# MoE of a sliding-window attention in 18 blocks of 256 tokens, two column tiles per slot; masks and relayouts of the first 16 slots on VectorE

## The chip, the cores and the metric

The kernel runs on one core of a Trainium2 chip. TensorE (PE) multiplies matrices into PSUM; VectorE (DVE), ScalarE (ACT) and GpSimd (POOL) work element by element; SyncE (SP) stores the output. Each engine carries out its own instructions in the order in which they were issued to it, and waits where an operand or a buffer isn't ready. The metric is the device time in microseconds (us); the kernel before takes 369.12 us, the median of three runs.

## What is computed

```python
# q, k, v: [8, 8, 576, 64] float32; w_in: [512, 2048]; w_out: [2048, 512]
scores = np.matmul(q, k.transpose(0, 1, 3, 2)) / np.sqrt(64)
scores = np.where(np.abs(pos[:, None] - pos[None, :]) <= 32, scores, -1e9)
attn   = softmax(scores)                       # over the last axis
x = np.matmul(attn, v).transpose(0, 2, 1, 3).reshape(4608, 512)
h = x @ w_in
g = np.where(h >= 1, h, np.where(h <= -1, 0.0, (h + 1) ** 2 / 4))
out = g @ w_out                                # [4608, 512] float32
```

There are 8 batches of 8 heads and 576 tokens. The window of 32 leaves, for each block of 64 keys, 128 queries (96 at the ends).

## The kernel before

**Attention.** Two heads of one batch are stacked on the 128 partitions and called a pair i (32 of them, four per batch); two pairs are loaded together and called m (16 of them, two per batch). GpSimd issues the loads, which also turn float32 into bfloat16: `load_qk(m)` for q and k, `load_v(m)` into a ring of four buffers vz. q, and k of m = 0 to 3 (`LONG = 4`), come in long rows; a copy (`relay`) then brings them into the order that TensorE's transposes want (tile qj or kj), `tpose(m, t)` transposes a part (t = 0, 1 for q, 2, 3 for k) into PSUM and copies it out as qT or kT, and for those k `zfill` copies kT into kz, where the two heads of a pair lie beside zeros. From m = 4 on, k is loaded by four DMAs of short runs in an order that needs neither: its transposes are copied from PSUM straight into kz, four copies by VectorE for each of t = 2 and 3.

`scores(i, g, eng)` does one of three groups of key blocks of a pair: matmuls (tile sc), ScalarE's exponential into pt, and a product with the band mask on the engine `eng`. `pv(i, half)` sums pt (tile dn) and multiplies it with vz (tile nm) for one half of 288 tokens, takes 1/dn as exp(-ln dn) on ScalarE, and leaves a product on VectorE for the next slot, which writes 288 columns of xT. Batch 0 is done for the first half before slot 0.

**MoE.** It runs in 9 blocks of TB = 512 tokens, each of 16 slots. A slot multiplies 128 rows of h, four matmuls of 512 columns, into PSUM (tile hp, two buffers); ScalarE makes rr = relu(h/2 + 1/2), VectorE the larger of hp and rr and then min(rr, 1) times that, which is g (tile gT). Block 0 alone takes its tokens in two halves of 256: its slots do two row tiles of 256 columns each. From slot 16 on every slot also does four matmuls of w_out for the block before (tile op, 16 of them sum up one output tile of 128 tokens, copied out by ScalarE and stored by SP). Sixteen slots at the end have only these.

**What sets the order.** It is written out by hand. A table `ev` says in which slot a score group ("s"), a transpose ("t") or a pv half ("v") stands; `loads` says in which slot GpSimd issues a load, and `rel` puts a relayout one slot ahead of its first transpose. Inside a slot the order is: loads, products left over from pv, hp and its three elementwise operations, scores, op, relayouts, transposes, zfill, pv. Up to slot 5 the masks are VectorE's, from slot 6 on GpSimd's (`eng = V if a < 6 else P`); all relayouts and refills inside the slots are GpSimd's. A GpSimd load waits for the load issued eight before it, and for its buffer.

Of the kernel before, what the change touches and what calls it, by code (L numbers as in the profile page):

```python
# [15 lines left out]
def kernel(  # L16
# [68 lines left out]

    LONG = 4

# [71 lines left out]
    load_qk(2)  # L159
    load_qk(3)  # L160
    load_v(2)


# [11 lines left out]
    def tpose(m, t, early=False):  # L175
# [26 lines left out]
    def zfill(m, g, early=False):  # L202
        for h in range(2):
            r = slice(64 * h, 64 * h + 64)
            copy = nc.gpsimd.tensor_copy if not early else nc.scalar.copy if h else nc.vector.tensor_copy
            copy(kz[2 * (m % 2) + g][r, :, h], kT[m][r, g].rearrange("d (c r) -> d c r", r=64))  # L206

    pt = {}

    def scores(i, g, eng):  # L210
# [108 lines left out]
    for n, a in enumerate([8, 9, 10, 11, 13, 14, 15, 15]):  # L319
        at(a, "v", 4 + n // 2, n % 2)  # L320
    for b in range(2, B):
        a0 = 16 * (b - 1)
        early = b == 2
        for n in range(4):
            for g in range(3):
                at(a0 + (1, 1, 2)[g] if early and n == 0 else a0 + 4 * n + g - 2, "s", 4 * b + n, g)
            at(a0 + 4 * n + 1 + (1 if early and n == 0 else 0), "v", 4 * b + n, 0)
            at(a0 + 4 * n + 3, "v", 4 * b + n, 1)
        for t in range(4):
            at((15, 15, 16, 16)[t] if early else a0 - 10 + 2 * t, "t", 2 * b, t)  # L330
            at(a0 + 1 + t if early else a0 - 2 + 2 * t, "t", 2 * b + 1, t)
    slots = sorted(set(ev) | set(range(16 * NB + 16)))
    rel, zf = {}, {}
    for a, es in ev.items():
        for e in es:
            if e[0] == "t" and (e[2] == 0 or e[2] == 2 and e[1] < LONG):
                rel.setdefault(slots[slots.index(a) - 1], []).append((e[1], e[2] // 2))
            if e[0] == "t" and e[2] == 3 and e[1] < LONG:
                zf.setdefault(a, []).append(e[1])
# [89 lines left out]
```

## Time and profile before

| | |
|---|---|
| median of 3 runs | 369.12 us (369.08 to 369.27) |
| profiled execution | 368.57 us, of which its span of instructions 366.8 us |
| TensorE busy | 323.5 us, 88% of the span |
| VectorE, ScalarE, GpSimd busy | 268.8, 226.4, 181.9 us |
| mean granted TensorE clock | 0.972 of 2.4 GHz |

A busy share is an average over stages with different limits, so the stages are read apart: the timeline of an engine shows when each operation starts, how long it takes, and behind which engine's work it waited; windows give the busy time of each engine in a stretch. The chain that ended last follows the end of the program back through what released each step. A granted clock of 0.50 is TensorE's lower level, 1.2 GHz.

### The profile page before, as it was taken

The numbers are of one execution on the slowest core, as the hardware profiler recorded it, in microseconds if no ns is written. First come the engines' busy times: TensorE is split into PE (matmuls) and PEld (weight loads), VectorE is DVE, ScalarE is ACT, GpSimd is POOL, SyncE is SP. The second block draws the span as 40 slices with busy tenths as digits, with TensorE's granted clock in tenths as the row PEclk, the third lists the DMA queues.
The fourth block names the chain that finished last, engine by engine and source line by source line (L and its number), as shares of the span: only waits on it lengthen the run. The fifth ranks groups of instructions, "written<-read, shape, count | busy, mean of one in ns | idle before, by whom it ended". The sixth has DMA issues, their size and how long they took to land.

```text
span 366.8 us, 6093 instructions
## 1 busy us (share of the span) xinstructions
PE 323.5 (88%) x2205; PEld 184.8 (50%) x2240; DVE 268.8 (73%) x489; ACT 226.4 (62%) x449; POOL 181.9 (50%) x229
## 2 busy tenths in 40 slices
PE   2577276488999999899999999999999999999995
PEld 1456165345555555455555555555555544444442
DVE  6569363556887888788888797979797788878810
ACT  7968354456776776677676868686866653443321
POOL 8935988939484849384949494824223200000000
PEclk9989878879999999999999999999999999999999
DMA  7999999759193949393929090900000011001012
GB/s 104 187 209 185 204 60 94 66 32 116 34 98 63 82 74 109 47 91 64 116 42 126 30 126 29 128 30 29 31 29 30 29 42 46 29 37 51 29 59 84
DMA packets 79612, 28.16 MB, mean 77 GB/s; under 512 B 66784, under 2 KB 74464, under 8 KB 79584
## 3 DMA queue, kind: packets, MB, share of 16 engines
q0 software_dynamic: 74400, 18.36, 53.6%
q1 hardware_dynamic: 5184, 9.44, 6.9%
q8 instruction: 17, 0.28, 0.3%
q14 instruction: 11, 0.09, 0.1%
HBM read 36.70 MB, written 9.44 MB: 126 GB/s over the span
## 4 chain that ended last, share of the span: by engine, by line
PE 77%; POOL 10%; ACT 4%; DVE 3%; issue 3%; DMA 2%; POOLq 0%; ACTq 0%
PE op L380 33%; PE hp L363 31%; PE tp L186 4%; PE nm L246 4%; PE sc L218 3%; POOL pt L223 3%; POOL kn L95 3%; PE dn L236 2%; PE dn L237 2%; DMA kn<-in_k_dram 2%; POOL kz L206 1%; POOL qn L100 1%; DVE pt L223 1%; POOL vz L105 1%; ACT rc L251 1%
## 5 line engine op out<-in xcount | busy, mean ns | idle before, releaser
L363 PE MATMUL hp<-xT,w_in 128*128 128x512 bf16 (+1 forms) x621 | 151.5, 366 | 3.5 <-DVE xT L255 2.2
L380 PE MATMUL op<-w_out,gT 128*128 128x512 bf16 x560 | 143.4, 380 | 0.9
L367 ACT ACTIVATE rr<-hp 128x512 f32<-128x512 f32 x144 | 86.0, 597 | 83.9 <-PE hp L363 72.9
L368 DVE TENSOR_TENSOR hp<-hp,rr 128x512 f32<-128x512 f32 x144 | 100.7, 699 | 45.7 <-ACT rr L367 43.7
L223 POOL TENSOR_TENSOR pt<-pt,maskp 128x352 bf16<-128x352 bf16 (+2 forms) x84 | 73.8, 884 | 94.5 <-ACT pt L222 94.3
L369 DVE SCALAR_TENSOR_TENSOR gT<-rr,hp 128x512 bf16<-128x512 f32 x144 | 99.0, 687 | 5.0
L363 PEld LDWEIGHTS <-w_in 128*128 128x128 bf16 x640 | 60.1, 101 | 42.8 <-issue 1.7
L380 PEld LDWEIGHTS <-gT 128*128 128x128 bf16 x576 | 53.5, 98 | 52.3 <-issue 1.3
L222 ACT ACTIVATE pt<-sc 128x352 bf16<-128x352 f32 (+2 forms) x96 | 44.0, 468 | 2.2 <-PE sc L218 2.1
L255 DVE TENSOR_TENSOR xT<-nm,rc 128x288 bf16<-128x288 f32 x64 | 29.0, 455 | 17.9 <-ACT rc L251 17.8
L250 ACT ACTIVATE lr<-dn 128x288 f32<-128x288 f32 x64 | 26.5, 414 | 18.6 <-PE dn L237 18.6
L218 PEld LDWEIGHTS <-kz 128*128 128x128 bf16 x288 | 23.2, 101 | 24.9 <-issue 4.9
L95 POOL DMA_DIRECT2D kn<-in_k_dram x48 | 35.7, 767 | 0.0
L218 PE MATMUL sc<-qT,kz 128*128 128x128 bf16 (+1 forms) x288 | 30.8, 222 | 4.9 <-ACT pt L222 2.7
L198 ACT COPY qT<-tp 128x640 bf16<-128x640 bf16 (+1 forms) x32 | 23.4, 741 | 12.9 <-PE tp L186 12.7
L384 ACT COPY osb<-op 128x512 f32<-128x512 f32 x36 | 21.1, 586 | 15.9 <-PE op L380 13.5
L105 POOL DMA_DIRECT2D vz<-in_v_dram x32 | 28.0, 886 | 5.8 <-DMA w_in<-in_moe_w_in_dram 5.8
L192 DVE COPY kz<-tp 64x320 bf16<-64x320 bf16 (+1 forms) x96 | 29.1, 304 | 1.1
L251 ACT ACTIVATE rc<-lr 128x288 f32<-128x288 f32 x64 | 28.5, 445 | 2.0
L236 PE MATMUL dn<-pt,ones 128*128 128x288 bf16 x64 | 18.9, 296 | 9.2 <-POOL pt L223 6.4
L246 PE MATMUL nm<-pt,vz 128*128 128x128 bf16 (+2 forms) x320 | 26.8, 216 | 0.1
L186 PE MATMUL tp<-ident,qj 128*128 128x128 bf16 x144 | 14.2, 236 | 13.9 <-DVE qj L170 7.5
(40 smaller groups left out, 165.6 us busy)
## 6 DMA issues: line engine op xcount, KB each, us to landing
out_dram<-osb SPq DMA_DIRECT2D x36, 256.0 KB, 2.0
qn<-in_q_dram POOLq DMA_DIRECT2D x16, 288.0 KB, 4.4
vz<-in_v_dram POOLq DMA_DIRECT2D x32, 144.0 KB, 4.4
kn<-in_k_dram POOLq DMA_DIRECT2D x48, 72.0 KB, 4.4
w_out<-in_moe_w_out_dram POOLq DMA_DIRECT2D x2, 1024.0 KB, 13.6
w_in<-in_moe_w_in_dram POOLq DMA_DIRECT2D x2, 768.0 KB, 12.1
kn<-in_k_dram POOLq DMA_DIRECT2D x4, 288.0 KB, 9.2
w_in<-in_moe_w_in_dram POOLq DMA_DIRECT2D x2, 256.0 KB, 6.8
```

Of the source, the lines that this page charges most:

```text
L95: nc.gpsimd.dma_start(out=t[64 * g:64 * g + 64, :, h], in_=src[b, 2 * qd + g + 4 * h].rearrange("(c r) d -> r c d", r=64))
L105: nc.gpsimd.dma_start(out=vz[m % 4][64 * h:64 * h + 64, :, :, 64 * h:64 * h + 64].rearrange("r g c d -> r (g c) d"), in_=v[b, 4 * h + 2 * ...
L218: nc.tensor.matmul(ps[:, off:off + q1 - q0], kz[2 * (m % 2) + gg][:, c].rearrange("d h r -> d (h r)"), qT[m][:, gg, q0:q1], start=True, st ...
L222: nc.scalar.activation(pt[i][:, seg], ps[:, :off], AF.Exp, scale=D ** -0.5)
L223: eng.tensor_mul(pt[i][:, seg], pt[i][:, seg], maskp[:, seg])
L246: nc.tensor.matmul(nm[:, q0 - lo:q1 - lo], vz[i // 2 % 4][:, i % 2, c], pt[i][:, pc(c, q0):pc(c, q0) + q1 - q0], start=n == 0, stop=n == l ...
L251: nc.scalar.activation(rc, lr, AF.Exp, scale=-1.0)
L363: nc.tensor.matmul(hp[:, n * j:n * j + n], w_in[:, kk, 128 * fi:128 * fi + 128], xT[:, kk, TB * t + cols.start:TB * t + cols.stop], start= ...
L367: nc.scalar.activation(rr, hp, AF.Relu, scale=0.5, bias=0.5)
L368: nc.vector.tensor_max(hp, hp, rr)
L369: nc.vector.scalar_tensor_tensor(gT[t][:, ff[0]:ff[-1] + 1, cols], rr.rearrange("p (f n) -> p f n", n=n), 1.0, hp.rearrange("p (f n) -> p ...
L380: nc.tensor.matmul(op, gT[t - 1][:, ff, 128 * tt:128 * tt + 128], w_out[:, ff], start=ff == 0, stop=ff == 15)
```

## The change

The MoE takes 18 blocks of 256 tokens (TB = 256), each of NF = 8 slots; every slot does two row tiles of 256 columns, as block 0's did, and op begins with block 1, at slot 8. There are still 144 slots with hp, and 8 behind them. Slots are numbered as before, so slot a of both has done the same amount of hp. k of m = 2 and 3 is loaded in the natural form too (`LONG = 2`), so `zfill` is left only ahead of slot 0; six buffers kz hold three m (index 2 * (m % 3) + g wherever kz is named), and for m < 4 ScalarE makes the copies of the second head. Masks up to slot 15 and the relayouts of q that stand in those slots (m = 2 to 5) are VectorE's. w_out is loaded right behind v of m = 2, ahead of q, k and v of m = 3, and the loads of m = 4 to 6 stand some slots earlier, v of m = 7 later. Batch 1's scores and pv spread over slots 6 to 18; those of batch 2 stand nearly as before.

```diff
-    qtp = ctx.enter_context(tc.tile_pool(name="qtp", bufs=2))
+    qtp = ctx.enter_context(tc.tile_pool(name="qtp", bufs=3))
...
-    gtp = ctx.enter_context(tc.tile_pool(name="gtp", bufs=2))
+    gtp = ctx.enter_context(tc.tile_pool(name="gtp", bufs=3))
...
-    kz = [const.tile([128, NC, 2, 64], BF, name=f"kz{i}") for i in range(4)]
+    kz = [const.tile([128, NC, 2, 64], BF, name=f"kz{i}") for i in range(6)]
...
-    LONG = 4
+    LONG = 2
...
     load_qk(2)
-    load_qk(3)
     load_v(2)
+    load_w_out(0)
+    load_w_out(1)
...
-                    nc.vector.tensor_copy(kz[2 * (m % 2) + g][r, j0:j1, h],
+                    copy = nc.scalar.copy if m < 4 and h else nc.vector.tensor_copy
+                    copy(kz[2 * (m % 3) + g][r, j0:j1, h],
...
-    TB = 512
+    TB = 256
     NB = NT // TB
+    NF = DFF // 256
...
-        at(5 + t, "t", 3, t)
-    for n, a in enumerate([6, 7, 8, 9, 9, 10, 11, 12, 12, 13, 14, 14]):
-        at(a, "s", 4 + n // 3, n % 3)
...
+        at(6 + t, "t", 3, t)
+    for n in range(4):
+        for g in range(2):
+            at(6 + 2 * n + g, "s", 4 + n, g)
+        at(8 + 2 * n, "v", 4 + n, 0)
+        at(14 + n, "s", 4 + n, 2)
+        at(15 + n, "v", 4 + n, 1)
...
-    loads = {1: [(load_v, 3)], 3: [(load_w_out, 0)], 4: [(load_w_out, 1)]}
+    loads = {0: [(load_qk, 3), (load_v, 3)]}
     for m in range(4, NP // 2):
-        loads.setdefault({4: 6, 5: 9, 6: 14}.get(m, 8 * m - 38), []).append((load_qk, m))
-        loads.setdefault({4: 8, 5: 11, 6: 16, 7: 18}.get(m, 8 * m - 37), []).append((load_v, m))
+        loads.setdefault({4: 3, 5: 8, 6: 12}.get(m, 8 * m - 38), []).append((load_qk, m))
+        loads.setdefault({4: 6, 5: 10, 6: 17, 7: 20}.get(m, 8 * m - 37), []).append((load_v, m))
...
-    for a in slots:
-        t, f = divmod(a, 16)
-        eng = V if a < 6 else P
+    for a in range(NF * NB + NF):
+        t, f = divmod(a, NF)
+        eng = V if a < 16 else P
...
-            hp = ps_h.tile([128, TB], FP, name="hp")
-            if t == 0:
-                hb, f = divmod(f, 8)
-                cols, ff, n = slice(256 * hb, 256 * hb + 256), (2 * f, 2 * f + 1), 256
-            else:
-                cols, ff, n = slice(0, TB), (f,), TB
-            for j, fi in enumerate(ff):
+                gT[t] = gtp.tile([128, 2 * NF, TB], BF, name="gT")
+            hp = ps_h.tile([128, 2, TB], FP, name="hp")
+            for j in range(2):
                 for kk in range(4):
-                    nc.tensor.matmul(hp[:, n * j:n * j + n], w_in[:, kk, 128 * fi:128 * fi + 128],
-                                     xT[:, kk, TB * t + cols.start:TB * t + cols.stop], start=kk == 0, stop=kk == 3)
+                    nc.tensor.matmul(hp[:, j], w_in[:, kk, 256 * f + 128 * j:256 * f + 128 * j + 128],
+                                     xT[:, kk, TB * t:TB * t + TB], start=kk == 0, stop=kk == 3)
...
-        for e in rel.get(a, []):
-            relay(*e, P)
+        for m in rel.get(a, []):
+            relay(m, 0, eng)
...
-        for m in zf.get(a, []):
-            for g in range(2):
-                zfill(m, g)
```

GpSimd's row, from q of m = 3 (before) or v of m = 2 (after) on. The names qn_170 and qn_359 are q of m = 3, kn_172 and kn_361 its k, vz2 and vz3 the v of m = 2 and 3. Before:

```order
L100 DMA qn_170<-in_q_dram 128x2x576
L100 DMA kn_172<-in_k_dram 128x2x576
L105 DMA vz2_111<-in_v_dram 64x18x64 x2
L105 DMA vz3_112<-in_v_dram 64x18x64 x2
L170 COPY qj_395<-qn_166 128x2x9x64
L116 DMA w_out_102<-in_moe_w_out_dram 128x8x512
L170 COPY kj_474<-kn_168 128x2x9x64
L116 DMA w_out_102<-in_moe_w_out_dram 128x8x512
L170 COPY qj_510<-qn_170 128x2x9x64
L206 COPY kz0_105<-kT_512 64x9x64 x2
```

After:

```order
L105 DMA vz2_113<-in_v_dram 64x18x64 x2
L116 DMA w_out_102<-in_moe_w_out_dram 128x8x512 x2
L100 DMA qn_359<-in_q_dram 128x2x576
L95 DMA kn_361<-in_k_dram 64x9x64 x4
L105 DMA vz3_114<-in_v_dram 64x18x64 x2
L100 DMA qn_466<-in_q_dram 128x2x576
L95 DMA kn_468<-in_k_dram 64x9x64 x4
L105 DMA vz0_111<-in_v_dram 64x18x64 x2
L100 DMA qn_629<-in_q_dram 128x2x576
L95 DMA kn_631<-in_k_dram 64x9x64 x4
L105 DMA vz1_112<-in_v_dram 64x18x64 x2
```

w_out stood behind the loads of m = 3, between relayouts; now it stands ahead of them, and no copy is left among the loads. vz0 and vz1 that follow belong to m = 4 and 5.

VectorE's row around slots 5 and 6. hp_534 and hp_551 are slot 5, hp_572 and hp_577 slot 6, hp_600 and hp_605 slot 7; qj_564 is the relayout of q of m = 3. Before:

```order
L255 TENSOR_TENSOR xT_104<-nm_521,rc_530 128x288
L368 TENSOR_TENSOR hp_534<-hp_534,rr_543 128x512
L369 SCALAR_TENSOR_TENSOR gT_352<-rr_543,hp_534 128x2x256
L368 TENSOR_TENSOR hp_572<-hp_572,rr_581 128x512
L369 SCALAR_TENSOR_TENSOR gT_352<-rr_581,hp_572 128x2x256
L368 TENSOR_TENSOR hp_600<-hp_600,rr_609 128x512
L369 SCALAR_TENSOR_TENSOR gT_352<-rr_609,hp_600 128x2x256
L200 COPY kT_618<-tp_619 128x128x5
```

After:

```order
L257 TENSOR_TENSOR xT_104<-nm_538,rc_547 128x288
L364 TENSOR_TENSOR hp_551<-hp_551,rr_560 128x512
L365 SCALAR_TENSOR_TENSOR gT_368<-rr_560,hp_551 128x512
L171 COPY qj_564<-qn_359 128x2x9x64
L194 COPY kz4_109<-tp_566 64x4x64
L194 COPY kz5_110<-tp_566 64x4x64
L364 TENSOR_TENSOR hp_577<-hp_577,rr_586 128x512
L365 SCALAR_TENSOR_TENSOR gT_368<-rr_586,hp_577 128x512
L225 TENSOR_TENSOR pt_590<-pt_590,maskp_100 128x352
L364 TENSOR_TENSOR hp_605<-hp_605,rr_614 128x512
L365 SCALAR_TENSOR_TENSOR gT_368<-rr_614,hp_605 128x512
```

The relayout qj_564, which was GpSimd's qj_510 above, now stands between the last operation of slot 5 and the first of slot 6, with two of the new kz copies behind it, and the masks pt_590 of pair 4 stand behind the slots' own operations.

GpSimd's row from the mask of slot 8 on, before; pt_585, pt_692 and pt_767 are the masks of pairs 4, 5 and 6:

```order
L223 TENSOR_TENSOR pt_585<-pt_585,maskp_100 128x480
L206 COPY kz2_107<-kT_618 64x9x64 x2
L206 COPY kz3_108<-kT_618 64x9x64 x2
L100 DMA qn_671<-in_q_dram 128x2x576
L95 DMA kn_673<-in_k_dram 64x9x64 x4
L223 TENSOR_TENSOR pt_692<-pt_692,maskp_100 128x352
L223 TENSOR_TENSOR pt_692<-pt_692,maskp_100 128x256
L223 TENSOR_TENSOR pt_692<-pt_692,maskp_100 128x480
L105 DMA vz1_110<-in_v_dram 64x18x64 x2
L223 TENSOR_TENSOR pt_767<-pt_767,maskp_100 128x352
L223 TENSOR_TENSOR pt_767<-pt_767,maskp_100 128x256
```

After, these masks are in VectorE's row; GpSimd's, from k of m = 6 (slot 12) on, has its first masks in slots 16 and 17:

```order
L95 DMA kn_786<-in_k_dram 64x9x64 x4
L225 TENSOR_TENSOR pt_732<-pt_732,maskp_100 128x480
L225 TENSOR_TENSOR pt_995<-pt_995,maskp_100 128x352
L105 DMA vz2_113<-in_v_dram 64x18x64 x2
L225 TENSOR_TENSOR pt_804<-pt_804,maskp_100 128x480
L225 TENSOR_TENSOR pt_995<-pt_995,maskp_100 128x256
L225 TENSOR_TENSOR pt_995<-pt_995,maskp_100 128x480
L100 DMA qn_1078<-in_q_dram 128x2x576
L95 DMA kn_1080<-in_k_dram 64x9x64 x4
L225 TENSOR_TENSOR pt_1099<-pt_1099,maskp_100 128x352
L225 TENSOR_TENSOR pt_1099<-pt_1099,maskp_100 128x256
```

Refills, loads and masks took turns on GpSimd from slot 8 on; now they begin to do so at slot 16 only, with loads and masks.

## Rows read from the trace of the kernel before

**Rows 1.** Windows: length, busy us (count) of each engine, clock, DMA share, GB/s.
```profile
20.00:75.80 55.80, 34.05 (x315) 27.58 (x314) 31.62 (x51) 30.52 (x65) 41.93 (x51) 0.84 1.19 132
...
91.40:291.00 199.60, 196.51 (x1396) 110.91 (x1420) 166.77 (x310) 141.55 (x290) 112.82 (x133) 1.00 0.56 66
```

**Rows 2.** Timeline of PE: start, us, operation, count, idle before and releaser.
```profile
45.53 0.71 PE L186 MATMUL tp<-ident,kj 128*128 128x128 bf16 x5 [5.54 <-POOL kj L170]
...
72.60 1.14 PE L186 MATMUL tp<-ident,qj 128*128 128x128 bf16 x9 [5.19 <-POOL qj L170]
```

**Rows 3.** Windows of 1 us, columns as in Rows 1; clock third from the end.
```profile
44.00:45.00 1.00, 0.00 (x0) 0.00 (x0) 0.00 (x0) 0.00 (x0) 1.00 (x2) 0.50 1.20 210
...
50.00:51.00 1.00, 1.00 (x7) 0.73 (x6) 0.55 (x2) 0.44 (x1) 0.94 (x3) 0.60 0.40 25
```

**Rows 4.** Timeline of PE, hp matmuls that begin slots 6, 16 and 22.
```profile
36.02 1.04 PE L363 MATMUL hp<-xT,w_in 128*128 128x256 bf16 x8
...
75.78 1.60 PE L363 MATMUL hp<-xT,w_in 128*128 128x512 bf16 x3 [0.22 <-issue]
...
94.68 1.03 PE L363 MATMUL hp<-xT,w_in 128*128 128x512 bf16 x3
```

**Rows 5.** Chain that ended last: start, us, what.
```profile
25.79 1.04 PE hp L363 x8
...
31.98 0.89 PE hp L363 x8
...
90.48 0.86 PE hp L363 x4
```

**Rows 6.** Timeline of DVE, columns as in Rows 2.
```profile
9.74 0.46 DVE L170 COPY qj<-qn 128x1152 bf16<-128x1152 bf16 x1 [0.25 <-DMA qn<-in_q_dram]
...
17.92 0.57 DVE L223 TENSOR_TENSOR pt<-pt,maskp 128x352 bf16<-128x352 bf16 x2 [2.29 <-ACT pt L222]
...
18.41 0.82 DVE L255 TENSOR_TENSOR xT<-nm,rc 128x288 bf16<-128x288 f32 x2
...
24.69 0.40 DVE L223 TENSOR_TENSOR pt<-pt,maskp 128x480 bf16<-128x480 bf16 x1
...
28.82 2.48 DVE L223 TENSOR_TENSOR pt<-pt,maskp 128x480 bf16<-128x480 bf16 x1
...
33.60 0.69 DVE L368 TENSOR_TENSOR hp<-hp,rr 128x512 f32<-128x512 f32 x1
...
34.93 0.82 DVE L200 COPY kT<-tp 128x640 bf16<-128x640 bf16 x1
...
79.38 2.60 DVE L192 COPY kz<-tp 64x320 bf16<-64x320 bf16 x8
```

**Rows 7.** Timeline of POOL, 14 to 31 us: load issues and a copy.
```profile
14.74 0.72 POOL L100 DMA_DIRECT2D qn<-in_q_dram  x1
...
16.85 0.72 POOL L100 DMA_DIRECT2D kn<-in_k_dram  x1
...
17.55 1.75 POOL L105 DMA_DIRECT2D vz<-in_v_dram  x2
...
25.93 0.85 POOL L105 DMA_DIRECT2D vz<-in_v_dram  x1 [3.46 <-DMA w_in<-in_moe_w_in_dram]
...
28.96 1.16 POOL L170 COPY kj<-kn 128x1152 bf16<-128x1152 bf16 x1
...
30.05 0.88 POOL L116 DMA_DIRECT2D w_out<-in_moe_w_out_dram  x1
```

**Rows 8.** DMA issues, landing us last; windows 14:15, 16.8:17.4, 25:26.5, 30:30.9.
```profile
qn<-in_q_dram POOLq DMA_DIRECT2D x1, 288.0 KB, 12.1
...
kn<-in_k_dram POOLq DMA_DIRECT2D x1, 288.0 KB, 14.3
...
vz<-in_v_dram POOLq DMA_DIRECT2D x1, 144.0 KB, 9.0
...
w_out<-in_moe_w_out_dram POOLq DMA_DIRECT2D x1, 1024.0 KB, 15.2
```

More of the change, by code (lines that the diff above doesn't have):

```diff
@@ L205, in zfill @@
             copy = nc.gpsimd.tensor_copy if not early else nc.scalar.copy if h else nc.vector.tensor_copy
-            copy(kz[2 * (m % 2) + g][r, :, h], kT[m][r, g].rearrange("d (c r) -> d c r", r=64))
+            copy(kz[2 * (m % 3) + g][r, :, h], kT[m][r, g].rearrange("d (c r) -> d c r", r=64))
     pt = {}
@@ L217, in scores @@
             q0, q1 = qrange(c)
-            nc.tensor.matmul(ps[:, off:off + q1 - q0], kz[2 * (m % 2) + gg][:, c].rearrange("d h r -> d (h r)"),
+            nc.tensor.matmul(ps[:, off:off + q1 - q0], kz[2 * (m % 3) + gg][:, c].rearrange("d h r -> d (h r)"),
                              qT[m][:, gg, q0:q1], start=True, stop=True)
@@ L315 @@
         at(2 + t, "t", 2, t)
-        at(5 + t, "t", 3, t)
-    for n, a in enumerate([6, 7, 8, 9, 9, 10, 11, 12, 12, 13, 14, 14]):
-        at(a, "s", 4 + n // 3, n % 3)
-    for n, a in enumerate([8, 9, 10, 11, 13, 14, 15, 15]):
-        at(a, "v", 4 + n // 2, n % 2)
+        at(6 + t, "t", 3, t)
[5 more added lines that the diff above has]
+        at(15 + n, "v", 4 + n, 1)
     for b in range(2, B):
@@ L325 @@
             for g in range(3):
-                at(a0 + (1, 1, 2)[g] if early and n == 0 else a0 + 4 * n + g - 2, "s", 4 * b + n, g)
+                at(a0 + (0, 1, 1)[g] if early and n == 0 else a0 + 4 * n + g - 2, "s", 4 * b + n, g)
             at(a0 + 4 * n + 1 + (1 if early and n == 0 else 0), "v", 4 * b + n, 0)
@@ L329 @@
         for t in range(4):
[L330 to L333, printed above, removed]
+            at(12 + t if early else a0 - 10 + 2 * t, "t", 2 * b, t)
+            at(a0 - 2 + 2 * t, "t", 2 * b + 1, t)
+    rel = {}
     for a, es in ev.items():
         for e in es:
[L336 to L339, printed above, removed]
-    loads = {1: [(load_v, 3)], 3: [(load_w_out, 0)], 4: [(load_w_out, 1)]}
+            if e[0] == "t" and e[2] == 0:
+                rel.setdefault(a - 1, []).append(e[1])
+    loads = {0: [(load_qk, 3), (load_v, 3)]}
     for m in range(4, NP // 2):
-        loads.setdefault({4: 6, 5: 9, 6: 14}.get(m, 8 * m - 38), []).append((load_qk, m))
-        loads.setdefault({4: 8, 5: 11, 6: 16, 7: 18}.get(m, 8 * m - 37), []).append((load_v, m))
+        loads.setdefault({4: 3, 5: 8, 6: 12}.get(m, 8 * m - 38), []).append((load_qk, m))
+        loads.setdefault({4: 6, 5: 10, 6: 17, 7: 20}.get(m, 8 * m - 37), []).append((load_v, m))
     gT, spare = {}, [False]
-    for a in slots:
-        t, f = divmod(a, 16)
-        eng = V if a < 6 else P
+    for a in range(NF * NB + NF):
+        t, f = divmod(a, NF)
+        eng = V if a < 16 else P
         for fn, m in loads.get(a, []):
@@ L351 @@
         flush()
-        if t < NB and a == int(a):
+        if t < NB:
             if f == 0:
-                gT[t] = gtp.tile([128, 16, TB], BF, name="gT")
-            hp = ps_h.tile([128, TB], FP, name="hp")
-            if t == 0:
-                hb, f = divmod(f, 8)
-                cols, ff, n = slice(256 * hb, 256 * hb + 256), (2 * f, 2 * f + 1), 256
-            else:
-                cols, ff, n = slice(0, TB), (f,), TB
-            for j, fi in enumerate(ff):
+                gT[t] = gtp.tile([128, 2 * NF, TB], BF, name="gT")
+            hp = ps_h.tile([128, 2, TB], FP, name="hp")
+            for j in range(2):
                 for kk in range(4):
-                    nc.tensor.matmul(hp[:, n * j:n * j + n], w_in[:, kk, 128 * fi:128 * fi + 128],
-                                     xT[:, kk, TB * t + cols.start:TB * t + cols.stop], start=kk == 0, stop=kk == 3)
-            rr = ewp.tile([128, TB], FP, name="rr")
+                    nc.tensor.matmul(hp[:, j], w_in[:, kk, 256 * f + 128 * j:256 * f + 128 * j + 128],
+                                     xT[:, kk, TB * t:TB * t + TB], start=kk == 0, stop=kk == 3)
+            rr = ewp.tile([128, 2, TB], FP, name="rr")
             nc.scalar.activation(rr, hp, AF.Relu, scale=0.5, bias=0.5)
             nc.vector.tensor_max(hp, hp, rr)
-            nc.vector.scalar_tensor_tensor(gT[t][:, ff[0]:ff[-1] + 1, cols], rr.rearrange("p (f n) -> p f n", n=n), 1.0,
-                                           hp.rearrange("p (f n) -> p f n", n=n), op0=ALU.min, op1=ALU.mult)
+            nc.vector.scalar_tensor_tensor(gT[t][:, 2 * f:2 * f + 2], rr, 1.0, hp, op0=ALU.min, op1=ALU.mult)
         es = ev.get(a, [])
@@ L374 @@
                 scores(e[1], e[2], eng)
-        if t >= 1 and a == int(a):
+        if t >= 1:
             for x in range(4 * f, 4 * f + 4):
-                tt, ff = divmod(x, 16)
+                tt, ff = divmod(x, 2 * NF)
                 if ff == 0:
@@ L380 @@
                 nc.tensor.matmul(op, gT[t - 1][:, ff, 128 * tt:128 * tt + 128], w_out[:, ff],
-                                 start=ff == 0, stop=ff == 15)
-                if ff == 15:
+                                 start=ff == 0, stop=ff == 2 * NF - 1)
+                if ff == 2 * NF - 1:
                     osb = osp.tile([128, DM], FP, name="osb")
@@ L391 @@
                 tpose(e[1], e[2])
-        for m in zf.get(a, []):
-            for g in range(2):
-                zfill(m, g)
         for e in es:
             if e[0] == "v":
-                pv(e[1], e[2], a < 16 and spare[0])
+                pv(e[1], e[2], a < NF and spare[0])
                 spare[0] = not spare[0]
```

## The prediction

> **What bounds the kernel now.** I read the stages first: between 20 and 75.8 us TensorE is busy for 34.05 of 55.80 us, between 91.4 and 291 us for 196.51 of 199.60 [rows 1]. So from about 91 us on the kernel is bound by TensorE's own work, and all that can be won lies before. The timeline of TensorE shows what the early gaps are: three waits of about 5 us, each ended by GpSimd; the first and the last stand here, 5.54 us for a relayout of k and 5.19 for one of q, and the one between them is for a mask [rows 2]. They have one cause: GpSimd carries out loads, relayouts, refills of kz and masks in one row, so a mask stands behind loads that it doesn't need. In such a gap the granted clock falls to 0.50, the lower level, and is back at full speed only at about 50.6 us, 5 us after TensorE resumed at 45.5 [rows 2, 3]. Slot 6 starts at 36.02, slot 16 at 75.78, slot 22 at 94.68 [rows 4].
>
> **The change part by part.**
>
> *Same work, other columns.* A slot now has eight hp matmuls of 256 columns in place of four of 512. Pieces of the chain that end when TensorE goes on show 0.89 us for eight and 0.86 us for four [rows 5]; with nothing waited for at either end the eight are about 0.87, so I take 0.0125 us more per slot, with 0 and 0.18 as ends (the other piece of eight lasts 1.04, but it ends with ScalarE taking the result, so it holds the way out of the array too). The Trainium skill, "TensorE: Matmul & The Clock Gate", section "Back-to-back issue gap", gives two rules: N / 2.4 + 2.5 ns for a matmul by itself, by which the split costs 4 x 2.5 = 10 ns a slot, 1.3 us over 128 slots (an estimate from that page); and a sustained 81 ns at 128 and 131 ns at 512 columns, by which an estimate for 256 lies between these, and the split costs 0.12 us a slot or more, 15 us and up. This trace has 0.86 / 4 = 215 ns for 512 columns in the sustained stretch, so the first rule holds here, and the second would only make the price of rival C likelier.
>
> *Block 0's outputs start at slot 8, not 16.* By slot 22 the new order has issued 14 x 4 op matmuls, the old one 6 x 4. These 32 x 0.215 = 6.9 us go from a stretch where TensorE is the bound into one where it waited. In the last block nothing else moves: the last output copy and its store stay.
>
> *m = 3 is loaded behind w_out.* Before, q of m = 2 landed at 14.74 + 12.1 = 26.84, k of m = 3 at 16.85 + 14.3 = 31.15, the last piece of v of m = 3 at 25.93 + 9.0 = 34.93, w_out's second half at 30.05 + 15.2 = 45.25 [rows 7, 8]. One after the other, so the differences price the queue: three row loads of 288 KB in 4.31, 1.44 each; two v pairs in 3.78, 1.89 a pair; w_out 10.32. Now the queue holds q2, then k2 in four pieces (64 partitions in short runs, like v, so 1.89; with 1.44 as the low end), v2, w_out, then q3: 26.84 + 1.89 + 1.89 + 10.32 + 1.44 = 42.4 us for q3. Its relayout is no longer on GpSimd: it stands in VectorE's row right behind slot 5's two operations, ahead of slot 6's. Before, slot 6 starts on TensorE at 36.02 [rows 4], with a mask of 2.48 us on the way [rows 6]; VectorE is up to a pair of operations behind TensorE, and that mask is 2 us shorter without GpSimd's copies, so I reach the relayout at 36.0, a microsecond either way. So VectorE stops from 36.0 to 42.4, and TensorE, which needs its result in slot 6, from about 35 to 42.9. This new wait is as long as any that goes. Queued behind it are slot 6's max and product, all later masks, and the hp buffers. The later loads follow at the same prices: k and v of m = 3 by 46.2, q and k of m = 4 by 49.5, v of m = 4 and q of m = 5 by 52.8. Their relayouts stand in slots 11 and 13, near 56 and 60 us by the sum below, so they cost nothing unless the queue slips by 7 us.
>
> *Slots 6 to 15, now free of GpSimd.* VectorE does 10 pairs at 1.33 (33.60 to 34.93), 8 masks of batch 1 as 4 x 0.49 (17.92 to 18.41, one of 352 and one of 256) and two of 480 at 0.40, 14 kz copies at 2.60 / 8 = 0.325, two relayouts at 0.46, five xT products at 0.41 [rows 6]: 13.3 + 2.0 + 0.8 + 4.6 + 0.9 + 2.1 = 23.7 us. TensorE has 50,944 columns, at 0.86 / 2048 = 0.42 ns [rows 5] 21.4 us. Neither hides the other wholly: taking the larger in each slot gives 1.6, 1.6, 2.7, 2.2, 2.4, 2.0, 2.7, 2.1, 3.4, 3.4 = 24.1 us. After a gap of 8 us the clock will be at 0.50 for some 5 us again; in these two light slots VectorE hides half of it, so 1.2 us more. Slot 16 then starts at 42.9 + 24.1 + 1.2 = 68.2. The masks on VectorE are bounded by 0.40 and by the 2.48 us of the one at 28.82, beside which GpSimd copied from 28.96 [rows 6, 7]; the two at 17.92, beside the issue of v that began at 17.55, took 0.57 together. Since GpSimd now only issues loads there, I take the low end. The Trainium skill, "SBUF — State Buffer", section "SBUF: two separate sides", says the same of the cause: the two engines share a port pair under a lock, and VectorE with two SBUF inputs is held only by a GpSimd operation that reads SBUF. By that rule the masks cost 0.40; without it, rival D.
>
> *Two k's more in the direct form* (LONG = 2): two relayouts of k and eight refills by GpSimd are gone; half of the kz copies that replace them is on ScalarE, six in these ten slots, about 2 us if they cost it what they cost VectorE, on an engine that waits for the other two; bounded by 0 and those 2. Two more kz buffers cost four VectorE memsets before slot 0, below 2 us even at a relayout's 0.46 each; slot 2 needs all of w_in, which lands about 25.9 [rows 7], and slot 5's relayout waits for q3, so nothing is left of them.
>
> *Slots 16 to 21.* Masks are back on GpSimd, between the loads of m = 6 and 7. TensorE has 35,904 columns, 15.1 us. Before, the same slots took 94.68 - 75.78 = 18.9 us for 14.0 us of columns, 4.9 lost, two of them to the clock. Now slot 18 holds two pv of one buffer in a row. I take 2.2 us of waits, with 0 and 4.9 as ends. Slot 22 starts at 68.2 + 15.1 + 2.2 = 85.5.
>
> *The rest.* Before, from slot 22 to the end of the span 366.8 - 94.68 = 272.1. Of that 6.9 goes and 122 x 0.0125 = 1.5 comes: 266.7. The span ends at 352.2; with the 1.77 us around it (368.57 less 366.8) the profiled execution would be 354.0, against 368.57. The median of the runs, 369.12, is 0.55 above that profile, so I predict 354.5.
>
> **The rivals.** A: the new wait doesn't come, because q3 lands by 36 (the loads share the queue instead of following each other). Then 6.9 and 1.2 us of the above are saved: 346.5. For it, only that landing times are ends of transfers; against it, the even spacing of those in [rows 7, 8].
> B: the middle stays slow. If VectorE, TensorE and ScalarE, all near full, hold each other up in slots 6 to 15, at 3.1 us a slot instead of 2.5 (before, slots 6 to 15 took 39.8 us, 4.0 each, with the three waits of 5 us in them), that is 5.8, and with the whole 4.9 lost in slots 16 to 21, 2.7 more: 363. For it: masks are on GpSimd again from 16 on, between two loads. Against it: in slots 6 to 15 no engine is full, and the masks from 16 on are asked for one to two slots ahead.
> C, slower: matmuls of 256 columns don't keep the pace, in every slot from 22 on. At the 1.04 of [rows 5], 0.165 a slot over what I took, 122 slots are 20.1 us: 374.6. It makes the kernel slower from 0.12 a slot on. Against it, the 0.89 of [rows 5]; for it, that each hp matmul now has its own weight load. The page's second rule above would be this case.
> D, slower too: the ten masks of slots 6 to 15 are held by GpSimd's issues as the one at 28.82 was by its copies, 2.08 each: 375. It needs 1.5 each to undo the gain; against it, the pair at 17.92.
>
> **How the numbers follow.** My forecast has 0.63, with 350 to 359 as its own range; A 0.10, B 0.21, C 0.04, D 0.02. About 0.2%, 0.7 us, is what a measurement of this kernel tells from no change. A, B and the forecast are faster, less 0.01 for B's far end within 0.2%: 0.93 faster, 0.01 same, and C and D 0.06 slower. The range takes in most of A, and B up to its value: 347.5 to 363.
>
> **What would show it.** Right: VectorE idle for about 6 us just before a relayout of q at 42 us, with that load as releaser; TensorE idle for 7 to 8 us there, and the clock at 0.50 behind it; no other gap above 2 us; slot 16 at 67 to 70 us with 32 op matmuls done; from slot 22 on TensorE as dense as before, 128-column pieces unchanged and eight hp matmuls at 0.87 to 0.89. Wrong: q3 in time (A); GpSimd as releaser of waits before slot 16, or masks on VectorE above 1 us (D); hp slots of 1.0 us in the dense stretch (C). If slot 16 comes after 72 us, the sum for slots 6 to 15 has failed; if it comes in time but the end doesn't, the step of the 32 op matmuls or of the columns has.

## The result, and the profile after

The changed kernel takes 357.87 us, the median of four runs (357.12 to 358.21), against 369.1 for the kernel before on the same chip: a ratio of 0.970, with an interval of 0.968 to 0.972. The profiled execution took 357.66 us, its span 355.8. Forecast were 354.5 with a range of 347.5 to 363, so it was faster as expected, by 3.7 us less than the sum said (354.0 for the profiled execution). TensorE is busy for 322.8 us, 91% of the span, in place of 88%.

The stages first, in windows of the kernel after: length, busy us of TensorE, weight loads, VectorE, ScalarE and GpSimd, granted clock, DMA share, GB/s. They run to the start of slot 16, to that of slot 22, and through the stretch behind it; the short ones follow the clock.

```profile
20.00:71.64 51.64, 37.70 (x342) 27.76 (x339) 34.53 (x75) 30.73 (x68) 22.50 (x29) 0.90 1.32 143
71.64:91.36 19.72, 15.98 (x158) 11.86 (x155) 14.47 (x32) 13.44 (x31) 15.56 (x18) 1.00 0.88 87
91.36:290.00 198.64, 198.64 (x1783) 146.34 (x1780) 166.61 (x307) 142.00 (x290) 110.38 (x132) 1.00 0.55 66
43.00:44.00 1.00, 0.00 (x0) 0.00 (x0) 0.28 (x1) 0.64 (x2) 1.00 (x2) 0.50 2.43 155
47.00:48.00 1.00, 1.00 (x7) 0.67 (x6) 0.86 (x2) 0.96 (x3) 1.00 (x2) 0.52 2.36 146
48.00:49.00 1.00, 1.00 (x10) 0.69 (x9) 0.73 (x2) 0.46 (x1) 1.00 (x3) 1.00 2.43 155
```

From slot 22 to 290 us the profile shows no idle time of TensorE at all, where 3.1 us were idle in the like stretch before [rows 1]. Slot 16 starts at 71.64 and slot 22 at 91.36, where it was 75.78 and 94.68 [rows 4]; and by then 56 op matmuls are done, where it was 24. TensorE is idle from 36.9 to 44.04; at the end of that the granted clock is at its lower level (0.50, 1.2 GHz), and it is back at 1.00 from 48 us on, 4 us after TensorE resumed (it was 5 [rows 3]).

The timeline of TensorE after: start, us, operation, count, and in brackets the idle time before it with its releaser. These are its first idle time, which answers to [rows 2], the starts of three slots, and the waits of slots 16 to 18.

```profile
44.04 0.69 PE L187 MATMUL tp<-ident,qj 128*128 128x128 bf16 x5 [7.16 <-ACT kz L194]
...
71.64 1.04 PE L359 MATMUL hp<-xT,w_in 128*128 128x256 bf16 x8
...
74.07 0.32 PE L220 MATMUL sc<-qT,kz 128*128 128x96 bf16 x3 [1.18 <-ACT pt L224]
...
77.98 0.37 PE L220 MATMUL sc<-qT,kz 128*128 128x128 bf16 x4 [0.85 <-ACT pt L224]
...
84.42 0.40 PE L248 MATMUL nm<-pt,vz 128*128 128x96 bf16 x5 [1.45 <-DVE xT L257]
...
86.98 1.04 PE L359 MATMUL hp<-xT,w_in 128*128 128x256 bf16 x8
87.85 0.37 PE L220 MATMUL sc<-qT,kz 128*128 128x128 bf16 x4
...
91.36 1.04 PE L359 MATMUL hp<-xT,w_in 128*128 128x256 bf16 x8
```

GpSimd ends no wait of TensorE any more; in place of three waits of 5 us there is one of 7.16. The chain of the kernel after tells what is behind it: start, us, what.

```profile
28.28 13.92 DMA qn<-in_q_dram
42.20 0.02 issue
42.22 0.46 DVE qj L171
42.68 0.20 DVE kz L194
42.88 0.02 issue
42.90 0.38 ACT kz L194
43.28 0.02 issue
43.30 0.29 DVE kz L194
43.60 0.02 issue
43.62 0.38 ACT kz L194
```

q of m = 3 lands at 42.20, as predicted (42.4). But TensorE doesn't go on with its relayout: four kz copies stand between, and they change hands three times. TensorE's wait ends with the last of them. VectorE's row of the kernel after shows the same turns in three places, ahead of VectorE's next operations (L257 of slots 5 and 9, L364 of slot 6):

```profile
34.95 0.31 DVE L194 COPY kz<-tp 64x320 bf16<-64x320 bf16 x1
35.74 0.32 DVE L194 COPY kz<-tp 64x320 bf16<-64x320 bf16 x1 [0.49 <-ACT kz L194]
37.45 0.46 DVE L257 TENSOR_TENSOR xT<-nm,rc 128x288 bf16<-128x288 f32 x1 [1.40 <-ACT rc L253]
...
42.22 0.46 DVE L171 COPY qj<-qn 128x1152 bf16<-128x1152 bf16 x1 [2.86 <-DMA qn<-in_q_dram]
42.59 0.28 DVE L194 COPY kz<-tp 64x256 bf16<-64x256 bf16 x1
43.30 0.28 DVE L194 COPY kz<-tp 64x256 bf16<-64x256 bf16 x1 [0.43 <-ACT kz L194]
44.64 0.70 DVE L364 TENSOR_TENSOR hp<-hp,rr 128x512 f32<-128x512 f32 x1 [1.06 <-ACT rr L363]
...
45.98 0.33 DVE L225 TENSOR_TENSOR pt<-pt,maskp 128x352 bf16<-128x352 bf16 x1
...
50.76 0.31 DVE L194 COPY kz<-tp 64x320 bf16<-64x320 bf16 x1
51.56 0.32 DVE L194 COPY kz<-tp 64x320 bf16<-64x320 bf16 x1 [0.49 <-ACT kz L194]
53.27 0.46 DVE L257 TENSOR_TENSOR xT<-nm,rc 128x288 bf16<-128x288 f32 x1 [1.40 <-ACT rc L253]
```

Each transposed tile costs VectorE 1.5 to 1.9 us of idle time: 0.4 to 0.5 until ScalarE's first copy is done, and 1.1 to 1.4 more because ScalarE's Ln, Exp or Relu, which VectorE wants next, stands behind its second.

### The profile page after: what moved, and what is told of

Read it like the earlier page. It is cut to its first block, busy times and chain, and to the rows that moved or that the text cites. A ratio compares the mean times of both kernels' runs of the same rounds, so it can differ in the third digit from the quotient of the medians.

```text
span 355.8 us, 7157 instructions
## 1 busy us (share of the span) xinstructions
PE 322.8 (91%) x2752; PEld 233.0 (65%) x2752; DVE 272.8 (77%) x513; ACT 227.7 (64%) x455; POOL 166.5 (47%) x211
## 4 chain that ended last, share of the span: by engine, by line
PE 79%; DMA 8%; DVE 5%; POOL 3%; ACT 3%; issue 2%; ACTq 0%; POOLq 0%
PE op L375 33%; PE hp L359 32%; DMA qn<-in_q_dram 4%; DMA w_in<-in_moe_w_in_dram 4%; PE nm L248 4%; PE tp L187 3%; PE sc L220 3%; PE dn L238 2%; PE dn L239 2%; DVE hp L364 1%; DVE gT L365 1%; DVE kz L194 1%; POOL vz L105 1%; ACT rr L363 1%; ACT kz L194 1%
## 5 line engine op out<-in xcount | busy, mean ns | idle before, releaser
L359 PE MATMUL hp<-xT,w_in 128*128 128x256 bf16 x1152 | 151.7, 275 | 1.6 <-DVE gT L365 1.2
L375 PE MATMUL op<-w_out,gT 128*128 128x512 bf16 x576 | 146.5, 379 | 0.0
L364 DVE TENSOR_TENSOR hp<-hp,rr 128x512 f32<-128x512 f32 x144 | 100.7, 699 | 40.9 <-ACT rr L363 38.0
L359 PEld LDWEIGHTS <-w_in 128*128 128x128 bf16 x1152 | 109.2, 99 | 21.6 <-DVE gT L365 1.9
L225 POOL TENSOR_TENSOR pt<-pt,maskp 128x480 bf16<-128x480 bf16 (+2 forms) x74 | 65.6, 889 | 101.9 <-ACT pt L224 101.7
L95 POOL DMA_DIRECT2D kn<-in_k_dram x56 | 41.8, 775 | 1.0 <-DVE qj L171 0.9
L257 DVE TENSOR_TENSOR xT<-nm,rc 128x288 bf16<-128x288 f32 x64 | 29.0, 455 | 14.1 <-ACT rc L253 12.3
L220 PE MATMUL sc<-qT,kz 128*128 128x128 bf16 (+1 forms) x288 | 30.9, 220 | 5.5 <-ACT pt L224 4.3
L252 ACT ACTIVATE lr<-dn 128x288 f32<-128x288 f32 x64 | 26.5, 414 | 13.7 <-PE dn L239 13.6
L194 DVE COPY kz<-tp 64x320 bf16<-64x320 bf16 (+1 forms) x104 | 31.4, 302 | 2.8 <-ACT kz L194 1.8
L187 PE MATMUL tp<-ident,qj 128*128 128x128 bf16 x144 | 14.4, 236 | 16.8 <-DVE qj L171 9.7
L187 PEld LDWEIGHTS <-qj 128*128 128x128 bf16 x144 | 11.3, 106 | 23.3 <-DVE qj L171 16.6
```

What stands on the lines that cost most here:

```text
L95: nc.gpsimd.dma_start(out=t[64 * g:64 * g + 64, :, h], in_=src[b, 2 * qd + g + 4 * h].rearrange("(c r) d -> r c d", r=64))
L187: nc.tensor.transpose(ps[:, j - j0], src[m][:, j].rearrange("p h d -> p (h d)"), ident)
L194: copy(kz[2 * (m % 3) + g][r, j0:j1, h], ps[r, :n].rearrange("d c (g r) -> d g c r", g=2)[:, g])
L220: nc.tensor.matmul(ps[:, off:off + q1 - q0], kz[2 * (m % 3) + gg][:, c].rearrange("d h r -> d (h r)"), qT[m][:, gg, q0:q1], start=True, st ...
L225: eng.tensor_mul(pt[i][:, seg], pt[i][:, seg], maskp[:, seg])
L359: nc.tensor.matmul(hp[:, j], w_in[:, kk, 256 * f + 128 * j:256 * f + 128 * j + 128], xT[:, kk, TB * t:TB * t + TB], start=kk == 0, stop=kk ...
```

## The experiments

The theory: what the sum lacks is this handing over of the kz copies, and the wait for q of m = 3 lies partly beneath it. The rivals: the load's wait is the whole of it; or slots 6 to 15 are slow because all engines are near full (rival B of the prediction). Ratios below are against the kernel before, run beside each; differences are between medians. The medians of the kernel before run from 368.9 to 369.5 us beside them, so a difference of half a microsecond tells nothing.

**q of m = 3 ahead of w_out.** The loads of slot 0 move up (`load_qk` gets an argument by which it loads q or k alone; that part is left out here):

```diff
+    load_qk(3, "q")
     load_w_out(0)
+    load_qk(3, "k")
     load_w_out(1)
+    load_v(3)
...
-    loads = {0: [(load_qk, 3), (load_v, 3)]}
+    loads = {}
```

> One edit to the changed kernel: q of m = 3 is loaded ahead of w_out's first half, its k between the two halves of w_out and its v behind them; nothing else moves. My theory: the wait for q of m = 3 (VectorE 2.86 us at 42.2, TensorE 7.16 us at 44.0) and the half clock behind it are paid in full, so with q landing near 32 us slot 7 begins near 37.5 instead of 44.5 and the kernel takes 349 to 352 us against 357.9. Rival: the wait only moves, because slots 8 to 10 then need w_out before it has landed, or because slots 6 to 15 are held by the engines' turns anyway; then the time is 355 us or more.

355.17 us, 0.960 (0.955 to 0.964): 2.7 us less, at the near end of the rival. Its trace, VectorE's row:

```profile
39.23 0.46 DVE L176 COPY qj<-qn 128x1152 bf16<-128x1152 bf16 x1
39.60 0.28 DVE L199 COPY kz<-tp 64x256 bf16<-64x256 bf16 x1
40.31 0.28 DVE L199 COPY kz<-tp 64x256 bf16<-64x256 bf16 x1 [0.43 <-ACT kz L199]
```

and TensorE's:

```profile
41.05 0.69 PE L192 MATMUL tp<-ident,qj 128*128 128x128 bf16 x5 [4.22 <-ACT kz L199]
```

The load is in time, VectorE no longer stands for it, and TensorE still waits 4.22 us. So my price was wrong. The rival's first reason isn't what the row shows, as no wait of TensorE ends with w_out; its second is, the turns that the engines take. Of the 4.22 us, 1.86 are left where nothing is shared (both edits together, below).

**All kz copies on VectorE.**

```diff
-                    copy = nc.scalar.copy if m < 4 and h else nc.vector.tensor_copy
+                    copy = nc.vector.tensor_copy
```

> One edit to the changed kernel: all four kz copies of a transpose of m = 2 and 3 are on VectorE, where two of the four are on ScalarE. My theory: the copies out of one transposed tile take turns between the engines and hold VectorE by 1.3 to 1.9 us each time (idle 0.43 and 1.06 at 43 to 45 us, 0.49 and 1.40 at 51 to 53, 0.43 and 1.05 at 55 to 57); with the turns gone, and 0.6 us of copies more on VectorE each time, slot 16 begins some 2.5 to 3 us earlier, near 69 us, and the kernel takes 354.5 to 356 us. Rival: TensorE or ScalarE sets the pace of slots 7 to 11, the idle time of VectorE costs nothing, and the added VectorE work makes it the same or up to 1.5 us slower: 357.5 to 359.5.

354.50 us, 0.958 (0.954 to 0.962): 3.4 us less, though VectorE has eight copies more to make. VectorE's row:

```profile
42.58 0.46 DVE L171 COPY qj<-qn 128x1152 bf16<-128x1152 bf16 x1 [4.88 <-DMA qn<-in_q_dram]
42.95 1.19 DVE L194 COPY kz<-tp 64x256 bf16<-64x256 bf16 x4
44.17 0.70 DVE L364 TENSOR_TENSOR hp<-hp,rr 128x512 f32<-128x512 f32 x1
```

Four copies in 1.19 us with nothing waited for behind them. VectorE now comes to the relayout at 37.7 and stands 4.88 us for the load. From the end of that wait (TensorE goes on at 43.09) to slot 16 (68.63) are 25.5 us; the prediction had 25.3, and with the handing over it was 27.6. The theory stands, at the near edge of what it gave.

**The order of the copies.** Two on VectorE, then two on ScalarE, the loops over g and h exchanged:

```diff
-            for g in range(2):
-                for h in range(2):
+            for h in range(2):
+                for g in range(2):
```

> On the changed kernel, the same two copies on VectorE and two on ScalarE, in another order: both of VectorE first, then both of ScalarE, so that there is one handover between the engines per transpose in place of three. My theory: the copies out of one tile go strictly one after another, so the order alone saves two handovers of about 0.1 us each and nothing else: the two ScalarE copies start only when both of VectorE's are done, Ln, Exp and Relu stand behind them as now, and it takes 357 to 358.3 us. Rival: it is the alternation itself that costs; then VectorE goes on after 0.6 us, and it takes 354 to 356 us.

357.07 us, 0.967 (0.965 to 0.970), at the lower edge of my theory, and 0.8 us below the changed kernel, with ranges that overlap. In ScalarE's row its two copies still wait for both of VectorE's (42.69 to 43.16):

```profile
43.25 0.64 ACT L194 COPY kz<-tp 64x256 bf16<-64x256 bf16 x2 [5.42 <-DVE kz L194]
43.91 0.60 ACT L363 ACTIVATE rr<-hp 128x512 f32<-128x512 f32 x1
```

It is not the alternation but the sharing of the transposed tile: in this kernel one engine reads it when the other is done, although they read different halves of its partitions. The tile kz that they write isn't it: VectorE's second copy waited for ScalarE's first, which goes into another kz. Nor is sharing a tile enough by itself. Ahead of slot 0 of the changed kernel, `zfill` has both engines copy halves of one kT, which lies in SBUF, into halves of one kz, and there they run at the same time:

```profile
11.51 1.24 ACT L208 COPY kz<-kT 64x576 bf16<-64x576 bf16 x2
...
11.53 0.79 DVE L208 COPY kz<-kT 64x576 bf16<-64x576 bf16 x2
```

The tile for which they take turns is one in PSUM.

**Whole transposes.** The first transposed tile of a k is copied by VectorE, the second by ScalarE:

```diff
-                    copy = nc.scalar.copy if m < 4 and h else nc.vector.tensor_copy
+                    copy = nc.scalar.copy if m < 4 and t == 3 else nc.vector.tensor_copy
```

> On the changed kernel, ScalarE keeps half of the kz copies of m = 2 and 3, but of whole transposes: all four copies of the first are VectorE's, all four of the second ScalarE's. My theory: no tile is shared, so VectorE and ScalarE each copy at their own pace; VectorE's idle time of 0.49 and 1.40 us at 35 and at 51 us goes, behind the second transposes the Relu still stands behind four copies of 0.37 on ScalarE, and it takes 355 to 357 us, between the changed kernel and that with all copies on VectorE (354.5). Rival: ScalarE's share costs whatever the order, since Ln, Exp and Relu stand behind it, and it takes 357.5 us or more.

353.97 us, 0.958 (0.955 to 0.960): better than I gave it. ScalarE makes as many copies as in the changed kernel, so its share of the work was not what cost. Its row, beside VectorE's four copies from 50.09 to 51.41:

```profile
52.01 1.50 ACT L194 COPY kz<-tp 64x256 bf16<-64x256 bf16 x4 [0.33 <-PE tp L187]
53.53 0.60 ACT L363 ACTIVATE rr<-hp 128x512 f32<-128x512 f32 x1
```

**Both waits taken away**: the first two edits together.

> The first two experiments together on the changed kernel: q of m = 3 loaded ahead of w_out, and all kz copies on VectorE. With q early alone, TensorE still waited 4.22 us at 41.05 for the kz copies; with the copies on VectorE alone, VectorE reached the relayout at 37.7 and stood 4.88 us for the load. My theory: the two waits cover each other, so each edit alone shows only part of its price, and together they give more than their sum (2.7 and 3.4 us): VectorE comes to the relayout at 37.7 with q there, 4.9 us before that of the second experiment, and with the half clock shortened the kernel takes 348 to 350.5 us. Rival: the two are worth their sum or less, because the load of w_out or of k now ends the next wait: 351.5 us or more.

349.18 us, 0.945 (0.943 to 0.948): 8.7 us below the changed kernel, where the two alone add up to 6.1. The traces agree: slot 16 starts 2.8 and 3.0 us earlier with one edit (68.83 and 68.63) and 8.9 with both (62.78). TensorE's row where the long wait was:

```profile
38.12 0.45 PE L192 MATMUL tp<-ident,qj 128*128 128x128 bf16 x5 [1.86 <-DVE qj L176]
```

Each wait hid part of the other. The load's wait is worth 2.7 us with the shared copies and 5.3 without them. The granted clock, from windows of this kernel, stays at 1.00 in 42 to 44 us, where it was 0.50:

```profile
42.00:44.00 2.00, 1.95 (x22) 1.54 (x22) 1.95 (x5) 1.44 (x4) 0.10 (x1) 1.00 1.44 189
```

**One pv out of slot 18**, in addition to the last:

```diff
-            at(a0 + 4 * n + 1 + (1 if early and n == 0 else 0), "v", 4 * b + n, 0)
+            at(a0 + 4 * n + 1 + (3 if early and n == 0 else 0), "v", 4 * b + n, 0)
```

> The kernel of the fifth experiment, and one pv more moved: the first half of pair 8 from slot 18, where it stands beside the second half of pair 7, to slot 20, which has none. My theory: the wait of TensorE in slot 18 (1.45 us for VectorE's product out of the one nm buffer, 0.26 for the one dn buffer) goes, and it takes 1.2 to 2 us less than the fifth. Rival: the wait moves to slot 19 or 21, because three pv then stand in slots 19 to 21, and the time is the same within 0.5 us.

348.14 us, 0.943 (0.940 to 0.945), 1.0 us less. The 1.45 and 0.26 of slot 18 are gone; slots 18 to 21 take 10.15 us (71.10 to 81.25) where they took 11.84 (70.67 to 82.51). Of these 1.7 us the medians show 1.0, with ranges that overlap, so the size is only roughly told; by the theory it would have been 1.2 or more.

**Masks back on GpSimd, alone**, from slot 6 on:

```diff
-                scores(e[1], e[2], eng)
+                scores(e[1], e[2], P if a >= 6 else V)
```

> One part of the change undone: from slot 6 on the masks are on GpSimd again, as before; relayouts stay on VectorE. My theory: GpSimd is busy issuing loads, with waits for room in the queue, until about 56.6 us, so the masks of slots 6 to 11 stand behind issues of 3.7 us and more, TensorE waits for them two or three times, and the kernel takes 360 to 364 us. Rival: the loads are far enough ahead and the masks are asked for a slot or two early, so it takes 356 to 358.5, and the whole gain comes from the block size and from the relayouts.

356.90 us, 0.966 (0.961 to 0.971); its runs (356.2 to 359.0) lie around those of the changed kernel. My theory fell: moving the masks was worth nothing here. While TensorE stood for q of m = 3, GpSimd issued its loads, and the masks came behind them.

**Masks back on GpSimd with both waits gone**, on the kernel with the moved pv:

> The kernel of the sixth experiment, and the masks of slots 6 to 15 back on GpSimd. The third experiment showed masks on GpSimd to cost nothing while TensorE stood waiting for q of m = 3. My theory: that was because the loads were issued by then; with everything 7 us earlier the masks of slots 8 to 12 stand behind the issues of loads that go on to about 56 us, and it takes 1 to 4 us more than the sixth. Rival: masks are asked for one to two slots ahead and VectorE is freed of 3 us of work, so it takes the same or up to 1 us less.

352.85 us, 0.956 (0.953 to 0.959): 4.7 us more than the same with the masks on VectorE, a little over my theory's 4. TensorE's row:

```profile
48.07 0.28 PE L243 MATMUL dn<-pt,ones 128*128 128x288 bf16 x1 [3.60 <-POOL pt L230]
```

and GpSimd's:

```profile
45.40 1.71 POOL L107 DMA_DIRECT2D vz<-in_v_dram  x2 [3.76 <-DMA w_out<-in_moe_w_out_dram]
47.17 1.48 POOL L230 TENSOR_TENSOR pt<-pt,maskp 128x352 bf16<-128x352 bf16 x2
```

GpSimd stood 3.76 us at a load of v until the second half of w_out, the load issued eight before it, had landed, and the masks of pair 4 stand behind that issue. So the move is worth 4.7 us once nothing longer covers it: the wait of 3.60, and the lower clock behind it (0.50 from 50 to 52 us).

**Masks and relayouts back on GpSimd**, on the changed kernel: the edit above, and

```diff
-            relay(m, 0, eng)
+            relay(m, 0, P)
```

> Both moves undone: masks from slot 6 on and all relayouts of the loop are on GpSimd; block size, column tiles and the direct loads of k stay. My theory: the relayouts add their own wait behind the issues, so this takes 1 to 4 us more than with the masks alone, 362 to 368 us, and GpSimd is the releaser of TensorE's waits between 35 and 75 us. Rival: the moves to VectorE are worth nothing, and block size, order of the outputs and direct k make the whole gain: 356 to 359 us.

366.24 us, 0.991 (0.989 to 0.994): 9.3 us above the masks alone, twice what I gave it and more. GpSimd's row, then TensorE's:

```profile
36.94 0.85 POOL L105 DMA_DIRECT2D vz<-in_v_dram  x1 [3.43 <-DMA w_out<-in_moe_w_out_dram]
37.83 1.14 POOL L171 COPY qj<-qn 128x1152 bf16<-128x1152 bf16 x1
```

```profile
39.03 0.71 PE L187 MATMUL tp<-ident,qj 128*128 128x128 bf16 x5 [10.46 <-POOL qj L171]
```

It is the relayout of m = 2, not that of 3, that stands behind the issues: TensorE waits for it from 28.6 to 39.0, mostly ahead of the stretch that my theory named; from there to 75 us no long wait of TensorE ends with GpSimd. The new order of loads, with w_out ahead of slot 0, is only to be had with the relayouts elsewhere.

**The relayouts alone, in the kernel before:** `relay(*e, P)` becomes `relay(*e, V)`. This moves every relayout inside the slots, those behind slot 15 too.

> The kernel before, with one part of the change alone: its relayouts are on VectorE instead of GpSimd; blocks of 512 tokens, masks and kz refills stay. My theory: the two waits of TensorE for relayouts on GpSimd (5.54 us at 45.5 and 5.19 at 72.6) go, the one for a mask (4.72 at 57.7) stays, the relayouts cost VectorE 0.46 us each, and it takes 358 to 362 us against 369: the move of the relayouts is the larger part of the change's gain. Rival: without the new block size GpSimd's refills and masks stand behind the loads as before, so the waits move to these, and it takes 366 us or more.

363.61 us, 0.984 (0.982 to 0.987): 5.9 us, where the whole change gave 11.2; between theory and rival. The two waits for relayouts are gone; those for masks grow, as the rival said. TensorE's row:

```profile
43.88 0.37 PE L236 MATMUL dn<-pt,ones 128*128 128x288 bf16 x1 [1.80 <-POOL pt L223]
...
54.70 0.40 PE L236 MATMUL dn<-pt,ones 128*128 128x288 bf16 x1 [5.64 <-POOL pt L223]
```

**The best of all**: q early, copies by whole transposes, pv moved.

> The three edits that paid, together: q of m = 3 ahead of w_out, kz copies of m = 2 and 3 by whole transposes (first VectorE, second ScalarE), the first half of pair 8 in slot 20. With all copies on VectorE the same took 348.1 us, and the split by transposes was 0.5 us below all on VectorE when alone. My theory: VectorE is now busy for nearly all of 34 to 52 us, so taking eight copies of 0.3 us off it shows in part: 346.5 to 348 us. Rival: ScalarE's four copies stand ahead of a Relu that TensorE waits for once the load is in time, and it is the same or up to 1.5 us slower: 348 to 349.7.

347.85 us, 0.942 (0.940 to 0.944), a span of 344.2 in the profiled execution. That is the kernel with all copies on VectorE (348.14) within their ranges, so it decides nothing between theory and rival; it stands 10.0 us below the changed kernel and 21 below the kernel before.

## Why the prediction was right, and what it mis-sized

*The direction and its cause: right.* The three waits for GpSimd went, and the slots behind 22 had nothing more to lose. GpSimd ends no wait of TensorE in the profile after.

*q of m = 3 behind w_out: right in time, wrong in price.* Landing at 42.20 for 42.4. But VectorE reached the relayout at 39.36, not 36.0. A shared transposed tile ahead of slot 5's operations made half of that: with all copies on VectorE it came at 37.70; the other 1.7 us are an estimate of VectorE's row that was too early. VectorE stood 2.86 us, not 6.4, and the load's wait is worth 2.7 us in this kernel. In the kernel that rival A described, with the load in time, the time would have been 355.2, not 346.5; the 8.1 us that A gave back are 5.3 even with the copies cured. TensorE's wait of 7.16 us is within the 7 to 8 that the prediction named, but by luck: it starts 1.9 us later than forecast, and ends 1.1 later, with the copies.

*Two k's more in the direct form: the step that failed.* The prediction bounded ScalarE's copies by 0 and 2 us, "on an engine that waits for the other two", and took nothing. It counted their busy time and not who shares what: here the two engines that read one transposed tile in PSUM waited for each other, and each held up all that stood behind it. That step measured 3.4 us (all copies on VectorE) to 3.9 (whole transposes). The sum was short by 3.7 us; slot 16 came 3.4 late, and the two misses behind it, below, are 2.4 too little and 2.3 too much, so they cancel by luck.

*Slots 6 to 15: the sum of 24.1 and 1.2 us holds* where nothing is shared (25.5 us with all copies on VectorE, 25.45 by whole transposes); in the changed kernel it was 27.6, and slot 16 came at 71.64 for 68.2. My mark for a right sum was 67 to 70 us and that for a failed one 72, so the time fell between them. Rival B's price (3.1 us a slot, 31 in all) wasn't reached. That the engines hold each other up was true, but not because they are full: VectorE took eight copies more and the stretch became shorter.

*Masks at 0.40: right.* Beside GpSimd's load issues from 45.65 to 47.40 the mask at 45.98 took 0.33 us, so rival D is refuted. By the Trainium skill, "SBUF — State Buffer", section "SBUF: two separate sides", a VectorE operation with two SBUF inputs is held only by a GpSimd operation that reads SBUF; this 0.33 us agrees if the issue of a load is none. That moving them pays nothing as long as the load's wait is there, I had not seen.

*Slots 16 to 21: 19.72 us for 17.3.* The waits of 1.18, 0.85, 0.26 and 1.45 us are 3.7, against the 2.2 taken; the whole is 4.6 above the columns, inside the ends of 0 and 4.9. The double pv in slot 18, which the prediction named, is the largest.

*The rest: 264.4 us for 266.7.* The 32 op matmuls moved as counted. The sum left the waits of the kernel before standing in this stretch. Two of them are at block boundaries, where TensorE waited 0.84 us each for VectorE's last columns of xT, at 118.45 and here at 154.75, in a view like [rows 2]:

```profile
154.75 0.38 PE L363 MATMUL hp<-xT,w_in 128*128 128x512 bf16 x1 [0.84 <-DVE xT L255]
```

No such wait is left in the kernel after; that a block of 256 needs fewer columns of xT at once is the likely reason, which no run tested. These two are 1.7 of the 2.3 us; the rest stays open.

*256 columns: right.* Eight hp matmuls take 0.87 us (86.98 to 87.85), 109 ns each. Rival C is refuted. So are, for this stream, the sustained figures of the Trainium skill, "TensorE: Matmul & The Clock Gate", section "Back-to-back issue gap", which the prediction had weighed; its formula, by which an estimate for eight is 0.873 us, agrees with the trace.

What stays open: what makes ScalarE's copies wait for VectorE's. The profile names the other engine's copy as releaser; whether the chip needs that wait or only the program asks for it, it doesn't tell. The Trainium skill, "PSUM — Partial Sum Buffer", section "PSUM bank collisions raise a hardware error", has two engines kept apart where they touch the same bank and the same group of 32 partitions, and says that different groups may be read at once. VectorE read partitions 0 to 63 here and ScalarE 64 to 127. By that rule they need not have waited, and the trace shows that they did; a kernel without that wait wasn't tried. Nor was the block size changed alone, so its share of the gain isn't known.

## What to carry to other kernels

Splitting the copies out of one PSUM tile over two engines didn't halve them: here they went in turns, and each engine's next work stood behind the other's last copy; so give each engine whole tiles. Where two waits lie over each other, one experiment prices neither: only the pair showed 8.7 us where the single ones showed 2.7 and 3.4, and a move (the masks) that was worth nothing became worth 4.7. When work is taken off the engine that issues loads, look at what the new order of loads makes late.

## What was not expected of the hardware

A load that must wait holds GpSimd's whole row, and here it waits for the load issued eight before it. With w_out's two halves among these, GpSimd stood 2.9 to 4.5 us at a load issue until a half had landed, and all that came next in its row stood with it. No run shows that the chip asks for this wait; it may be the program's alone.

The order of copies out of one tile counts even on one engine. Two of VectorE's from the same half of the partitions took 0.47 us together (the experiment on the order of the copies), less than twice the 0.28 of one alone. Four in which the halves take turns took 1.19 (all copies on VectorE), no less than four times 0.28. Why, no run here shows.
